# Another order of the setup, and three smaller moves, in a fused attention and expert kernel

## The chip, the cores and the metric

One core of one Trainium2 chip runs the whole kernel. The metric is the device time of one execution in microseconds (us). The kernel before was timed in three runs: 333.94, 334.50 and 335.64 us, median 334.5.

## The reference

There are two stages, and the output of the first is the input of the second.

Attention with a decaying state: 4 batches, 8 heads, 768 tokens, head size 48. For each head, token after token,

```python
cur   = outer(u * k[t], v[t])
y[t]  = r[t] @ (state + cur)
state = w[:, None] * state + outer(k[t], v[t])
```

Mixture of experts on the 3072 tokens with 384 features: logits are `x @ w_gate + modality_bias[modality_id]`; each token goes to the one expert with the largest logit, and gets `gate_w * (relu(x @ w1[e]) @ w2[e])`, with 8 experts of 384 x 1024 and 1024 x 384.

## The kernel before

**Units.** The 768 tokens of a batch are cut into six chunks of 128. A unit is one chunk of one batch; there are 24, numbered so that the four batches of one chunk follow each other. Within a unit the heads are held as four pairs. The state passes from a unit to the one four later.

**What a unit does.** With powers of w in two tables (`powr`, `powk`), GpSimd makes `rc = r * powr` (`decay`, L361) and the state's keys `kt` (`carry`, L368), VectorE makes `kc = k * powk` (`keys`, L399). TensorE multiplies them into 128 x 128 scores per head (`scores`, L440), VectorE multiplies the scores by the causal mask in two halves (`causal`, L454), and TensorE makes y from them and from v, and the state's increment (`values`, L472). The term of u is apart: `rk` is r times k (`own_turned` L393 for units 0 to 3, `own_keys` L383 later), TensorE multiplies it by u (`bonus`, L406) into a number d per token and head, which is copied out of PSUM (`taken`, L415), and d times v is the term `dv` (`own`, L430: eight ScalarE products, in two halves of four heads). For the units in `SHARED` (9 to 13) GpSimd makes the second half of `dv` in one product (`shared`, L423). VectorE adds `dv` to y (`add`, L506), ScalarE squares the sum for a scale (`token`, L512), VectorE makes a power of two of it (`factor`), ScalarE writes the scaled fp16 copy (`high`, L560) and VectorE the rest (`low`, L564). For units in `TURNED`, k is loaded only by token and TensorE transposes it (`keys_turned`, L348).

**Order.** Each engine has one queue and runs it in program order; the order is written out by hand. In iteration i of the main loop (L1266) the work of several units is interleaved: scores of unit i+1, values of unit i, the state copies (or additions) and the addition to y of unit i-1, causal products of i+1, decay of i+3, keys and state keys of i+2. Between them `fill()` takes single steps of longer jobs: gate weights, routing of finished token groups, the list of experts. `plan(i, f)` puts f at the end of iteration i, `mid[i]` between the two halves of `own`. SyncE issues nearly all loads in program order; some wait until a certain number is there (`pace`), so that the loads of later units and the first expert's weights (`raw`, in halves of six pieces, `half`) keep step with the units. A piece is squared for its scale when it has come (`norm`, L972, on ScalarE).

From unit 15 on (`EASED`) the state is added by VectorE, which then also copies d (units 15 and 16; from 17 on d comes by another way, `OWNED`).

**The setup (L85 to L201)** loads the first units, blanks the rows of the buffers that pad each 48 to 64, builds the tables of powers (copy of w L147, scan L148, reciprocals, copies on ScalarE L155 to L159), makes unit 0's operands (L164 to L168), and brings units 0 to 2 to the point where the loop begins. TensorE first multiplies ones (`WARM`, L135), and three more such products stand ahead of unit 1's scores (L446). `blank` (L106) writes zeros by ScalarE.

**The experts.** While the units run, the first expert's weights are brought to two fp16 halves, and tokens that are already routed go through it in slots. After the last unit a loop works through the rest in blocks of 128 tokens. TensorE has hardly a gap from there to the end.

Of the kernel before, what the change touches and what calls it, by code (L numbers as in the profile page):

```python
# [67 lines left out]
class _Kernel:  # L68
# [16 lines left out]
    def setup(self):  # L85
# [4 lines left out]
        nc.sync.dma_start(w[LOW:TOP, :], self.wT.rearrange("j d a -> (j d) a"))  # L90
        uT = c.tile([P, NPR], F32, name="uT")
        self.ud = [c.tile([P, 2 * NPR * P], F32, name=f"ud{q}") for q in range(4)]
# [30 lines left out]
        for i in range(3):  # L123
            self.lines(i, 1)
        wg = c.tile([P, DC * E], F32, name="wgf")
        nc.sync.dma_start(wg, self.wg)
        bias = c.tile([P, 2 * E], F32, name="bias")
        nc.sync.dma_start(bias, self.bias.to_broadcast([P, 2 * E]))
        mod = c.tile([P, 2 * NT // P], I32, name="mod")
        nc.sync.dma_start(mod, self.mod)  # L130
        self.raw_in = wg, bias, mod

# [6 lines left out]
        self.ones = c.tile([P, P], F32, name="ones")  # L139
        nc.vector.memset(self.ones, 1.0)  # L140
# [20 lines left out]
        p64 = pw[:, :, H2 : H2 + 1].rearrange("p a o -> p (a o)")  # L161
        nc.vector.tensor_mul(self.w128, p64, p64)
        self.ub, self.uw = (c.tile([P, NPR, 2], F32, name=n) for n in ("ub", "uw"))
        self.decay(0, NPR, NPR // 2)  # L164
        self.keys(0, 2)
        u = self.ctx_[0]
        nc.vector.tensor_mul(u["rc"][:TOP, NPR // 2 :], u["rT"][:TOP, NPR // 2 :], self.powr[:TOP, NPR // 2 :])
        self.own_turned(0)  # L168
# [16 lines left out]
        nc.gpsimd.memset(self.ub, 0.0)  # L185
        for j, r in enumerate(HALVES):
            nc.gpsimd.tensor_copy(self.ub[r, :, j], uT[r])
        self.keys_turned(1)
        self.causal(0, 0)
        self.causal(0, 1)  # L190
        self.keys(1)
        self.own_turned(1)
# [3 lines left out]
        pst = self.ps_s.tile([P, 512], F32, tag="s", name="psd")  # L196
        self.bonus(0, pst)
        self.taken(0)
        self.carry(1)
        self.feed(3)  # L200
        self.turned(4)  # L201

    def setup2(self):
# [48 lines left out]
    def counts(self):  # L252

        c, v = self.c, self.nc.gpsimd
        self.onesb = c.tile([P, P], BF16, name="onesb")
        v.memset(self.onesb, 1.0)
        self.id16 = c.tile([P, P], F16, name="id16")
        make_identity(self.nc, self.id16)
        self.tok = c.tile([P, NT // P], I32, name="tok")
# [7 lines left out]
        self.base = c.tile([P, E], F32, name="base")  # L267
        v.tensor_copy(self.base, self.cbase)
        self.line = c.tile([P, 1], F32, name="line")
        v.tensor_copy(self.line, self.tok[:, 0:1])  # L270

# [56 lines left out]

    def turned(self, i):
# [5 lines left out]
        self.nc.sync.dma_start(ud[LOW:TOP, :m], self.pd[b * NCH + c].rearrange("j d n -> (j d) n")[:, :m])  # L335
        self.ctx_.setdefault(i, {}).update( rT=ud[:, :n].rearrange("p (a t) -> p a t", a=NPR), kT=ud[:, n:].rearrange("p (a t) -> p a t", a=NPR))
# [23 lines left out]

    def decay(self, i, n=1, of=None):  # L361
        nc, u = self.nc, self.ctx_[i]
        u["rc"] = self.a.tile([P, NPR, P], F32, tag="rc", name=f"rc{i}", bufs=4)
        for q in range(of or n):
            s = slice(q * NPR // n, (q + 1) * NPR // n)
            nc.gpsimd.tensor_mul(u["rc"][:TOP, s], u["rT"][:TOP, s], self.powr[:TOP, s])  # L366

# [24 lines left out]

    def own_turned(self, i):  # L393

        u = self.ctx_[i]
        u["rk"], u["uw"] = self.a.tile([P, NPR, P], F32, tag="rk", name=f"rk{i}"), self.ub
        self.nc.vector.tensor_mul(u["rk"][:TOP], u["kT"][:TOP], u["rT"][:TOP])

    def keys(self, i, n=1):  # L399
        nc, a, u = self.nc, self.a, self.ctx_[i]  # L400
        u["kc"] = a.tile([P, NPR, P], F32, tag="kc", name=f"kc{i}")
        for q in range(n):
            s = slice(q * NPR // n, (q + 1) * NPR // n)
            nc.vector.tensor_mul(u["kc"][:TOP, s], u["kT"][:TOP, s], self.powk[:TOP, s])

# [34 lines left out]
    def scores(self, i):  # L440
        nc, u = self.nc, self.ctx_[i]
        u["ps"] = [self.ps_a.tile([P, 512], F32, tag="big", name=f"psc{i}_{j}") for j in range(2)]
        if i == 1:

            for q in range(DENSE // 2):
                nc.tensor.matmul(u["ps"][q % 2], self.ones16, self.warm, start=True, stop=True)  # L446

        for pr in range(NPR):
            for q in range(2):
                s = slice(64 * q, 64 * q + 64)  # L450
                for j, r in enumerate(HALVES):
                    nc.tensor.matmul(u["ps"][j][s, pr * P : (pr + 1) * P], u["kc"][r, pr, s], u["rc"][r, pr, :], start=True, stop=True)  # L452
# [519 lines left out]
    def norm(self, junk, q):  # L972
        self.nc.scalar.activation(junk, self.raw[:, q * WQ : (q + 1) * WQ], AF.Square, accum_out=self.ssq[:, q : q + 1])
# [191 lines left out]
    def run(self):  # L1165
# [26 lines left out]
        def plan(step, f):  # L1192
            at.setdefault(step, []).append(f)
# [72 lines left out]
        for i in range(NU - 1):  # L1266
            self.step = i
            if i == 0:
                each(i + 5, self.turned)
                each(i + 4, self.lines)  # L1270
            if i < GROUPED:
                each(i + 2, self.keys_turned)
# [336 lines left out]
```

## Time and profile before

| | |
|---|---|
| median of three runs | 334.5 us (333.94 to 335.64) |
| the profiled execution, its own time | 336.65 us |
| its span, first to last instruction | 334.6 us |
| mean granted TensorE clock | 0.994 |
| TensorE busy (products) | 320.0 us, 96% |
| VectorE, ScalarE, GpSimd busy | 213.5, 181.7, 159.7 us |

In a profile a line such as "row L562 <- DVE sx L318" says that the instruction of line 562 that writes the tile row waited, and that VectorE's line 318 released it. PE is TensorE's products, PEld its weight loads, DVE VectorE, ACT ScalarE, POOL GpSimd, SPq SyncE's queue of transfers. "issue" is time in which an engine waited for nothing that the profile shows. The setup and the first iterations take the first 14 us, iteration 4 begins near 26 us, the units end near 170 us.

### The profile page before, as it was taken

The page shows a single profiled execution, that of the slowest core. Times are in us where ns is not written, and L with a number is a line of the kernel's source. Part 1 is how long each engine was busy: PE and PEld are TensorE (multiplying, and loading weights), DVE is VectorE, ACT ScalarE, POOL GpSimd, SP SyncE. Part 2 cuts the span into 40 slices and gives each one's busy share as a digit, 9 for nine tenths or more (in the row PEclk, how much of TensorE's full clock was granted, in tenths as well). Part 3 has the DMA queues.
Part 4 walks back from the last instruction along what each step waited for, and adds up shares of the span by engine and source line. Part 5 has one row for each costly group of instructions (what it writes and reads, how often), then busy time and mean ns, then how long its engine had stood idle before and what let it go on. Part 6 is the DMA issues. An engine that isn't in the chain of part 4 may idle for free. (4 is left out here: it accounts for less than half of the span.)

```text
span 334.6 us, 15202 instructions
## 1 busy us (share of the span) xinstructions
PE 320.0 (96%) x5434; PEld 263.5 (79%) x5434; DVE 213.5 (64%) x727; ACT 181.7 (54%) x500; POOL 159.7 (48%) x241
## 2 busy tenths in 40 slices
PE   7999998998999999999999999999999999999992
PEld 2888897898978888797878788886888877777771
DVE  6878985899988988896667422286333332234950
ACT  7898888789655578676422222274222225543820
POOL 8978863967599886554458212203111111111211
PEclk9999999899999999999999999999999999999999
DMA  6879986995579999954246431119512211122110
GB/s 185 244 171 207 204 250 222 293 229 155 126 197 270 267 223 299 275 156 119 78 106 231 156 78 47 47 47 332 121 50 65 50 47 24 47 56 62 37 47 5
DMA packets 58013, 48.71 MB, mean 146 GB/s; under 512 B 42344, under 2 KB 50807, under 8 KB 57712
## 3 DMA queue, kind: packets, MB, share of 16 engines
q1 hardware_dynamic: 54768, 38.63, 47.5%
q0 software_dynamic: 3200, 9.47, 8.2%
q8 instruction: 30, 0.49, 0.7%
q14 instruction: 15, 0.12, 0.1%
HBM read 27.99 MB, written 11.83 MB: 119 GB/s over the span
## 5 line engine op out<-in xcount | busy, mean ns | idle before, releaser
L1067 PEld LDWEIGHTS <-whi 128*128 128x128 f16 x1248 | 72.6, 98 | 3.6 <-issue 0.7
L1076 DVE SCALAR_TENSOR_TENSOR hl<-phb,hh 128x256 f16<-128x256 f32 (+1 forms) x48 | 24.4, 508 | 66.8 <-ACTq L1540 66.8
L1130 PEld LDWEIGHTS <-hh 128*128 128x128 f16 x416 | 39.1, 98 | 25.3 <-ACT hh L1071 1.2
L1067 PE MATMUL phb<-mxT,whi 128*128 128x128 f16 x768 | 50.7, 219 | 0.0
L438 ACT ACTIVATE dv<-kv,d 128x48 f32<-128x48 f32 x172 | 43.0, 325 | 0.0
L1071 ACT ACTIVATE hh<-phb 128x256 f16<-128x256 f32 (+1 forms) x48 | 21.5, 455 | 32.4 <-PE phb L1067 22.9
L1067 PEld LDWEIGHTS <-wlo 128*128 128x128 f16 x624 | 37.8, 98 | 0.0
L1036 POOL TENSOR_TENSOR seenb<-otb,putb 128x1 int32<-128x1 int32 x16 | 4.1, 257 | 63.0 <-ACTq L1540 50.8
L458 DVE TENSOR_TENSOR at<-psc,mask 128x512 f32<-128x512 f32 x48 | 32.5, 681 | 1.5 <-PE psc L452 1.4
L1130 PEld LDWEIGHTS <-hl 128*128 128x128 f16 x208 | 19.8, 98 | 15.7 <-issue 2.5
L366 POOL TENSOR_TENSOR rc<-ud,powr 112x512 f32<-112x512 f32 (+1 forms) x25 | 30.8, 1237 | 0.2
L1027 ACT ACTIVATE otb<-po,fac 128x384 f32<-128x384 f32 x16 | 9.3, 580 | 39.5 <-PE phb L1067 39.5
L452 PE MATMUL psc<-rc,kc 64*64 64x128 f32 (+1 forms) x768 | 28.5, 281 | 1.2 <-POOL rc L366 1.0
L701 POOL DMA_INDIRECT rows<-row,posi x24 | 24.6, 1026 | 10.2 <-issue 3.6
L1067 PE MATMUL phb<-mxT,wlo 128*128 128x128 f16 x384 | 29.3, 219 | 0.0
L1130 PE MATMUL po<-whi,hl 128*128 128x384 f16 x136 | 28.0, 326 | 1.2 <-PEq L1605 0.7
L1130 PE MATMUL po<-whi,hh 128*128 128x384 f16 x136 | 27.7, 326 | 0.6 <-ACT hh L1071 0.4
L489 PE MATMUL py<-kv,at 128*64 128x48 f32 x768 | 27.0, 222 | 1.2 <-issue 1.2
L1067 PE MATMUL phs<-mxT,whi 128*128 128x128 f16 x432 | 27.3, 219 | 0.6 <-issue 0.6
L1130 PE MATMUL po<-wlo,hh 128*128 128x384 f16 x136 | 27.7, 326 | 0.0
L452 PEld LDWEIGHTS psc<-rc,kc 64*64 64x64 f32 (+1 forms) x768 | 21.9, 135 | 6.5 <-issue 2.5
L489 PEld LDWEIGHTS py<-kv,at 128*64 128x64 f32 x768 | 25.3, 138 | 2.1 <-issue 1.8
(292 smaller groups left out, 625.6 us busy)
## 6 DMA issues: line engine op xcount, KB each, us to landing
kv<-in_pt SPq DMA_DIRECT2D x21, 384.0 KB, 4.8
ud<-in_pd SPq DMA_DIRECT2D x14, 384.0 KB, 5.4
raw<-in_w SPq DMA_DIRECT2D x12, 256.0 KB, 5.1
raw<-in_w SPq DMA_DIRECT2D x6, 512.0 KB, 5.2
raw<-in_w SPq DMA_DIRECT2D x2, 1536.0 KB, 6.5
rows<-pad SPq DMA_DIRECT2D x10, 193.0 KB, 3.6
ud<-in_pd SPq DMA_DIRECT2D x10, 192.0 KB, 3.8
rt<-in_pt SPq DMA_DIRECT2D x7, 192.0 KB, 5.2
```

The costliest lines, as they stand in the source:

```text
L366: nc.gpsimd.tensor_mul(u["rc"][:TOP, s], u["rT"][:TOP, s], self.powr[:TOP, s])
L438: nc.scalar.activation(u["dv"][:, sl], u["v"][:, sl], AF.Copy, scale=u["d"][:, h : h + 1])
L452: nc.tensor.matmul(u["ps"][j][s, pr * P : (pr + 1) * P], u["kc"][r, pr, s], u["rc"][r, pr, :], start=True, stop=True)
L458: nc.vector.tensor_mul(u["at"][:, j * NPR : (j + 1) * NPR, :], u["ps"][j].rearrange("p (q t) -> p q t", q=NPR), self.mask.unsqueeze(1).to_ ...
L489: nc.tensor.matmul(py[t, sl], u["at"][:, j * NPR + pr, t], u["v"][:, sl], start=c == h == 0, stop=h == H - 1, skip_group_check=True)
L701: i = nc.gpsimd.indirect_dma_start(out=self.rows, out_offset=bass.IndirectOffsetOnAxis(ap=u["posi"][:, b : b + 1], axis=0), in_=u["row"][: ...
L1027: self.nc.scalar.activation(ot, po[:, :DM], AF.Copy, scale=gf[:, t : t + 1])
L1036: i1 = nc.gpsimd.tensor_tensor(seen, ot[:, 0:1].bitcast(I32), idx, ALU.add)
L1067: self.nc.tensor.matmul(ph[:, q * P : (q + 1) * P], w[:, c0 : c0 + P], self.xT[:, xq, t * P : (t + 1) * P], start=i == q == 0, stop=i == l ...
L1071: self.nc.scalar.activation(self.hh[:, f0 : f0 + fb, t * P : (t + 1) * P], p3, AF.Relu)
L1076: self.nc.vector.scalar_tensor_tensor(self.hl[:, f0 : f0 + fb, r], p3, 0.0, self.hh[:, f0 : f0 + fb, r], ALU.max, ALU.subtract)
L1130: self.nc.tensor.matmul(po[:, :DM], h[:, f, t * P : (t + 1) * P], w[:, c0 : c0 + DM], start=first, stop=last)
```

## The change

In the setup, unit 0's load is issued from ScalarE's queue, and the load of u becomes four rows of 96, which TensorE transposes and ScalarE copies to `ub` (before: 4-byte elements by the DMA, copies by GpSimd). Some memsets change their engine: `ud[0]` from VectorE to ScalarE, `ud[2]` from ScalarE to GpSimd, `ones` from VectorE to GpSimd. The `kt` blankings move ahead of the tables on ScalarE; those of `ud[3]` and of the state `st[1]` move behind the copy of unit 0's d. Unit 0's operands are made in a new function `first`; `rk` of unit 0 goes to GpSimd. Bonus and d of unit 0 and the transposition for unit 2 move ahead of the setup's end. The loads of the gate weights, bias and modality numbers go behind those of unit 3 (gate) and of unit 4's r (the other two). One warm-up product fewer, and the three ahead of unit 1's scores are left out. Unit 0's scores go through the pairs in the order 0, 1, 3, 2.

Besides: units 1 to 3 join `SHARED`; the squares of the second raw piece go from the end of iteration 8 to the middle of iteration 9; and in units 15 and 16 the copy of d stands ahead of the addition to y.

```diff
-WARM = 10
+WARM = 9
-DENSE = 6
-SHARED = range(9, 14)
+SHARED = (*range(1, 4), *range(9, 14))
...
         self.ones16 = warm[:, :P]
+        self.turned(0, nc.scalar)
+        self.turned(1)
+        ux = c.tile([NPR, TOP], F32, name="ux")
+        self.ub, self.uw = (c.tile([P, NPR, 2], F32, name=n) for n in ("ub", "uw"))
+        nc.gpsimd.memset(ux, 0.0)
+        nc.gpsimd.memset(self.ub, 0.0)
+        nc.sync.dma_start(ux[:, LOW:], self.u.rearrange("o (a z) -> (o a) z", a=NPR))
         for t in self.kv:
             nc.vector.memset(t[:, :LOW], 0.0)
-        nc.vector.memset(self.ud[0][:LOW], 0.0)
...
-        nc.vector.memset(uT, 0.0)
-        blank(self.ud[2][:LOW])
-        self.turned(0)
-        self.turned(1)
-        nc.sync.dma_start(uT[LOW:TOP, :], self.u.rearrange("o (a z) -> z (o a)", a=NPR))
+        blank(self.ud[0][:LOW])
+        for t in self.kt:
+            nc.scalar.copy(t[:, :, :LOW], zero[:, : NPR * LOW].rearrange("p (a z) -> p a z", a=NPR))
...
-        self.counts()
+        nc.gpsimd.memset(self.ud[2][:LOW], 0.0)
+        self.numbers()
...
+        self.first(p64)
         self.decay(1)
+        self.own_turned(0, nc.gpsimd)
         self.scores(0)
...
-        blank(self.ud[3][:LOW])
-        for t in self.kt:
-            nc.scalar.copy(t[:, :, :LOW], zero[:, : NPR * LOW].rearrange("p (a z) -> p a z", a=NPR))
+        self.masks()
+        psd = self.ps_s.tile([P, 512], F32, tag="s", name="psd")
+        nc.tensor.transpose(psd[:TOP, :NPR], ux, id32[:NPR, :NPR])
+        for j, r in enumerate(HALVES):
+            nc.scalar.copy(self.ub[r, :, j], psd[r, :NPR])
+        self.keys_turned(1)
...
+        self.causal(0, 0)
+        self.keys(1)
+        self.causal(0, 1)
+        self.own_turned(1)
+        self.keys_turned(2)
+        self.bonus(0, psd)
+        self.taken(0)
+        blank(self.ud[3][:LOW])
         blank(self.st[1].rearrange("p b a e -> p (b a e)"))
...
+        self.counts()
         self.feed(3)
+        wg = c.tile([P, DC * E], F32, name="wgf")
+        nc.sync.dma_start(wg, self.wg)
         self.turned(4)
+        bias = c.tile([P, 2 * E], F32, name="bias")
+        nc.sync.dma_start(bias, self.bias.to_broadcast([P, 2 * E]))
+        mod = c.tile([P, 2 * NT // P], I32, name="mod")
+        nc.sync.dma_start(mod, self.mod)
+    def first(self, p64):
...
+        part(nc.gpsimd, "rc", "rT", self.powr, slice(NPR - 1, NPR))
+        part(nc.vector, "kc", "kT", self.powk, lo)
+        part(nc.vector, "rc", "rT", self.powr, lo)
+        nc.vector.tensor_mul(self.w128, p64, p64)
+        part(nc.vector, "kc", "kT", self.powk, hi)
+        part(nc.vector, "rc", "rT", self.powr, slice(half, NPR - 1))
...
-        if i == 1:
-            for q in range(DENSE // 2):
-                nc.tensor.matmul(u["ps"][q % 2], self.ones16, self.warm, start=True, stop=True)
-        for pr in range(NPR):
+        for pr in range(NPR) if i else (0, 1, 3, 2):
...
-        for q in range(3):
+        for q in range(0, 3, 2):
             plan(O - 1 + q, norm(q))
+        mid[O + 1] = norm(1)
...
             if i >= EASED:
                 for j in range(2):
                     self.state(i - 1, j)
+                if i not in OWNED:
+                    self.taken(i)
             self.token(i - 1) if i else None
...
-            if i >= EASED:
+            if i in OWNED:
                 self.taken(i)
-                self.shared(i)
```

## Rows read from the trace of the kernel before

**Rows 1.** The page: engines (busy us, share, instructions), queues (packets, MB, share).
```profile
PE 320.0 (96%) x5434; PEld 263.5 (79%) x5434; DVE 213.5 (64%) x727; ACT 181.7 (54%) x500; POOL 159.7 (48%) x241
...
q8 instruction: 30, 0.49, 0.7%
```

**Rows 2.** Timeline of the setup, all but ScalarE: start us, us, engine, line, tiles, count.
```profile
1.27 0.94 POOL L104 MEMSET ud<- 16x1024 f32 x1
...
4.79 1.85 SPq L345 DMA_DIRECT2D kv<-in_pt  x4
...
5.70 2.73 POOL L366 TENSOR_TENSOR rc<-ud,powr 112x128 f32<-112x128 f32 x3
...
6.40 0.45 PE L452 MATMUL psc<-rc,kc 64*64 64x128 f32 x8 [0.56 <-POOL rc L366]
7.25 0.89 PE L452 MATMUL psc<-rc,kc 64*64 64x128 f32 x24 [0.41 <-POOL rc L366]
...
9.09 0.63 PE L413 MATMUL psd<-ub,rk 112*64 112x2 f32 x16
...
10.14 0.81 PE L446 MATMUL psc<-warm 128*128 128x512 f16 x3
...
10.35 1.27 POOL L366 TENSOR_TENSOR rc<-ud,powr 112x512 f32<-112x512 f32 x1
```

**Rows 3.** Timeline of the setup, ScalarE; in brackets the idle time before.
```profile
2.10 1.04 ACT L106 COPY ud<-zero 16x1024 f32<-16x1024 f32 x1
...
4.86 0.41 ACT L159 COPY powr<-powk 128x256 f32<-128x256 f32 x1
...
7.28 0.68 ACT L179 COPY kt<-zero 128x64 f32<-128x64 f32 x4
...
9.14 1.48 ACT L106 COPY st<-zero 128x1536 f32<-128x1536 f32 x1
10.51 0.17 ACT L421 COPY d<-psd 128x8 f32<-128x8 f32 x1
...
14.00 0.64 ACT L544 COPY st<-pst 64x192 f32<-64x192 f32 x2 [1.16 <-PE pst L413]
```

**Rows 4.** Timeline of iterations 1 to 4, all engines.
```profile
17.94 0.56 DVE L510 TENSOR_TENSOR py<-py,dv 128x384 f32<-128x384 f32 x1
...
18.53 0.49 ACT L529 ACTIVATE row<-py 128x384 f16<-128x384 f32 x1
...
19.30 1.28 POOL L391 TENSOR_TENSOR rk<-rc,kc 112x512 f32<-112x512 f32 x1
...
26.55 1.10 PE L452 MATMUL psc<-rc,kc 48*64 48x128 f32 x30 [0.23 <-DVE at L458]
```

**Rows 5.** Line 345, the loads by token, up to 16 us.
```profile
DMA to landing us min/median/max: 3.5/4.5/4.8
```

**Rows 6.** Timeline of iteration 9, 52 to 56 us, all engines.
```profile
53.50 1.06 ACT L973 ACTIVATE junk<-raw 128x1024 f16<-128x1024 f32 x1 [1.42 <-DMA raw<-in_w]
...
54.72 0.55 PE L489 MATMUL py<-kv,at 128*64 128x48 f32 x11 [1.17 <-issue]
...
55.41 0.48 PEld L497 LDWEIGHTS pst<-st,wd 112*64 112x64 f32 x15 [0.27 <-ACT d L421]
...
55.44 0.51 POOL L428 TENSOR_TENSOR dv<-kv,d 128x192 f32<-128x192 f32 x1 [4.77 <-ACT d L421]
```

**Rows 7.** Queues from 51.5 to 53.6 us: packets, MB, share of 16 engines.
```profile
q8 instruction: 1, 0.02, 5.9%
```

**Rows 8.** Timeline of iteration 15, 96.9 to 99 us.
```profile
98.06 0.64 PE L502 MATMUL pst<-kv,kt 128*64 128x48 f32 x16 [0.57 <-DVE d L421]
...
98.73 0.37 PEld L413 LDWEIGHTS pst<-uw,rk 112*64 112x64 f32 x10 [0.16 <-POOL rk L391]
```

**Rows 9.** Stretches (us): length, busy time (count) of each engine, PEclk, DMA share, GB/s.
```profile
5.80:6.40 0.60, 0.04 (x2) 0.01 (x1) 0.60 (x2) 0.60 (x4) 0.60 (x2) 1.00 1.01 331
...
57.20:60.60 3.40, 3.40 (x43) 3.01 (x42) 2.46 (x9) 3.36 (x10) 3.17 (x4) 0.50 0.80 222
```

More of the change, by code (lines that the diff above doesn't have):

```diff
@@ L90, in setup @@
         nc.sync.dma_start(w[LOW:TOP, :], self.wT.rearrange("j d a -> (j d) a"))
-        uT = c.tile([P, NPR], F32, name="uT")
         self.ud = [c.tile([P, 2 * NPR * P], F32, name=f"ud{q}") for q in range(4)]
@@ L124, in setup @@
             self.lines(i, 1)
[L125 to L131, printed above, removed]
         pt = self.ps_a.tile([P, 512], F32, tag="big", name="pwarm")
@@ L139, in setup @@
         self.ones = c.tile([P, P], F32, name="ones")
-        nc.vector.memset(self.ones, 1.0)
+        nc.gpsimd.memset(self.ones, 1.0)
         id32 = self.id32 = c.tile([P, P], F32, name="id32")
@@ L161, in setup @@
         p64 = pw[:, :, H2 : H2 + 1].rearrange("p a o -> p (a o)")
[L162 to L168, printed above, removed]
+        self.first(p64)
         self.decay(1)
+        self.own_turned(0, nc.gpsimd)
         self.scores(0)
@@ L183, in setup @@
         nc.scalar.copy(self.wtok, pt.rearrange("p (a z) -> p a z", a=NPR)[:, :, LOW:TOP])
-        blank(self.st[1].rearrange("p b a e -> p (b a e)"))
[L185 to L192, printed above, removed]
+        self.causal(0, 0)
[6 more added lines that the diff above has]
+        blank(self.ud[3][:LOW])
+        blank(self.st[1].rearrange("p b a e -> p (b a e)"))
         self.carry(0)
@@ L195, in setup @@
         nc.gpsimd.tensor_mul(self.uw, self.ub, w.unsqueeze(2).to_broadcast([P, NPR, 2]))
-        pst = self.ps_s.tile([P, 512], F32, tag="s", name="psd")
-        self.bonus(0, pst)
-        self.taken(0)
         self.carry(1)
+        self.counts()
         self.feed(3)
+        wg = c.tile([P, DC * E], F32, name="wgf")
+        nc.sync.dma_start(wg, self.wg)
         self.turned(4)
+        bias = c.tile([P, 2 * E], F32, name="bias")
+        nc.sync.dma_start(bias, self.bias.to_broadcast([P, 2 * E]))
+        mod = c.tile([P, 2 * NT // P], I32, name="mod")
+        nc.sync.dma_start(mod, self.mod)
+        self.raw_in = wg, bias, mod
+    def first(self, p64):
+        nc, u, half = self.nc, self.ctx_[0], NPR // 2
+        u["rc"] = self.a.tile([P, NPR, P], F32, tag="rc", name="rc0", bufs=4)
+        u["kc"] = self.a.tile([P, NPR, P], F32, tag="kc", name="kc0")
+        part = lambda eng, out, x, pw, s: eng.tensor_mul(u[out][:TOP, s], u[x][:TOP, s], pw[:TOP, s])
+        lo, hi = slice(0, half), slice(half, NPR)
+        part(nc.gpsimd, "rc", "rT", self.powr, slice(NPR - 1, NPR))
[4 more added lines that the diff above has]
+        part(nc.vector, "rc", "rT", self.powr, slice(half, NPR - 1))
     def setup2(self):
@@ L254, in counts, with masks @@
         c, v = self.c, self.nc.gpsimd
+        self.base = c.tile([P, E], F32, name="base")
+        v.tensor_copy(self.base, self.cbase)
+        self.line = c.tile([P, 1], F32, name="line")
+        v.tensor_copy(self.line, self.tok[:, 0:1])
+    def masks(self):
+        c, v = self.c, self.nc.gpsimd
         self.onesb = c.tile([P, P], BF16, name="onesb")
@@ L258, in counts, with numbers @@
         make_identity(self.nc, self.id16)
+    def numbers(self):
+        c, v = self.c, self.nc.gpsimd
         self.tok = c.tile([P, NT // P], I32, name="tok")
@@ L266, in counts @@
         self.idx, self.rev, self.cbase = (ci[:, q] for q in range(3))
[L267 to L270, printed above, removed]
     def setup5(self):
@@ L327, in feed, with turned @@
         self.lines(i)
-    def turned(self, i):
+    def turned(self, i, by=None):
         b, c = self.units[i]
@@ L334, in turned @@
         m = n if i in TURNED else 2 * n
-        self.nc.sync.dma_start(ud[LOW:TOP, :m], self.pd[b * NCH + c].rearrange("j d n -> (j d) n")[:, :m])
+        (by or self.nc.sync).dma_start(ud[LOW:TOP, :m], self.pd[b * NCH + c].rearrange("j d n -> (j d) n")[:, :m])
         self.ctx_.setdefault(i, {}).update( rT=ud[:, :n].rearrange("p (a t) -> p a t", a=NPR), kT=ud[:, n:].rearrange("p (a t) -> p a t", a=NPR))
@@ L359, in pace, with decay @@
         self.nc.values_load(ap[:1].bitcast(I32)[:, :1], engines=SP, skip_runtime_bounds_check_because="the value is not used, only the time at which it is there")
-    def decay(self, i, n=1, of=None):
+    def decay(self, i):
         nc, u = self.nc, self.ctx_[i]
         u["rc"] = self.a.tile([P, NPR, P], F32, tag="rc", name=f"rc{i}", bufs=4)
-        for q in range(of or n):
-            s = slice(q * NPR // n, (q + 1) * NPR // n)
-            nc.gpsimd.tensor_mul(u["rc"][:TOP, s], u["rT"][:TOP, s], self.powr[:TOP, s])
+        nc.gpsimd.tensor_mul(u["rc"][:TOP], u["rT"][:TOP], self.powr[:TOP])
     def carry(self, i):
@@ L391, in own_keys, with own_turned, keys @@
         nc.gpsimd.tensor_mul(u["rk"][:TOP], u["rc"][:TOP], u["kc"][:TOP])
-    def own_turned(self, i):
+    def own_turned(self, i, by=None):
         u = self.ctx_[i]
         u["rk"], u["uw"] = self.a.tile([P, NPR, P], F32, tag="rk", name=f"rk{i}"), self.ub
-        self.nc.vector.tensor_mul(u["rk"][:TOP], u["kT"][:TOP], u["rT"][:TOP])
-    def keys(self, i, n=1):
+        (by or self.nc.vector).tensor_mul(u["rk"][:TOP], u["kT"][:TOP], u["rT"][:TOP])
+    def keys(self, i):
         nc, a, u = self.nc, self.a, self.ctx_[i]
         u["kc"] = a.tile([P, NPR, P], F32, tag="kc", name=f"kc{i}")
-        for q in range(n):
-            s = slice(q * NPR // n, (q + 1) * NPR // n)
-            nc.vector.tensor_mul(u["kc"][:TOP, s], u["kT"][:TOP, s], self.powk[:TOP, s])
+        nc.vector.tensor_mul(u["kc"][:TOP], u["kT"][:TOP], self.powk[:TOP])
     def bonus(self, i, pst):
@@ L1270, in run @@
                 each(i + 4, self.lines)
-            if i < GROUPED:
+            if 0 < i < GROUPED:
                 each(i + 2, self.keys_turned)
```

## The prediction

> **What bounds the kernel now.** I read the page first. TensorE is busy for 96% of the span [rows 1], so the time follows its queue from the first scores to the last product, and an edit is worth only what it takes out of TensorE's waits. Second came the timeline of the setup: TensorE's first scores start at 6.40 us, wait again until 7.25, and from there the queue is nearly closed [rows 2]. Third came the timeline from 14 to 27 us, because TensorE looks full there and yet is led. One chain passes from ScalarE to VectorE and back with no slack: the state of unit 0 (14.00) [rows 3], `high(0)`, `low(0)`, `causal(2)`, the addition of unit 1 (17.94), its squares (18.53), `high(1)`, `low(1)`, `causal(3)`, the addition of unit 2, `causal(4)`, and then TensorE's scores of unit 5, which had waited for it (26.55) [rows 4]. So what a faster setup is worth at 26.55 is what it takes off 14.00, the start of the state copies, and not what it takes off the first scores. Behind 26.55 TensorE's waits are short, up to the two places that the last parts of the change touch.
>
> **The setup.** Three things change for the start of that chain.
>
> First scores. ScalarE gets the issue of unit 0's load ahead of its work, about 0.45 us (four issues of SyncE took 1.85) [rows 2], then the blanking of `ud[0]`, which takes the place of the one that starts at 2.10 and lasts 1.04, then the four `kt` copies (0.68) that stood at 7.28 [rows 3]. The tables can be copied from 2.10 + 0.45 + 1.04 + 0.68 - 0.2 (each starts about 0.1 before the one ahead ends) = 4.1. With three copies of 0.41 `powr` is whole at 5.1 to 5.3, against 4.86 + 0.41 = 5.27 before [rows 3]. What VectorE saves ahead of its scan (a memset of the shape that takes GpSimd 0.94 [rows 2], above all) is not passed on: ScalarE comes to the tables at 4.1 in any case. The gain is in what follows: VectorE itself multiplies r of the first two head pairs, and TensorE starts at about 5.7 instead of 6.40, without the second wait of 0.41 [rows 2].
>
> Unit 0's bonus. It needs three things. GpSimd: its queue ahead of the decays loses four small instructions and a wait and gains a memset of 0.94; I take it to be free when `powr` is there (5.2) or, at worst, at the 5.70 of before. The three products there took 2.73; now it is a whole one of 1.27 more and a quarter less, so 3.2, which gives 8.4 to 9.0 [rows 2]. The lines of unit 2: issued 0.5 to 1.0 earlier than 4.79 (unit 0's issue has left SyncE's queue, and the load of u waits for less), landed 3.5 to 4.8 after that [rows 5], and then a transposition of 10.14 - 9.09 - 0.63 = 0.4: 7.7 to 9.5. TensorE itself: 9.09 - 6.40 - 0.41 = 2.28 us of work from the first scores to the bonus before [rows 2], and the transpositions of unit 2 and of u besides, 0.6: 5.7 + 2.9 = 8.6. I take 8.6, which lies between all three, and keep 8.3 and 9.2 as ends.
>
> State of unit 0. In the profile ScalarE copied d at 10.51, was done with its eight products and the gate's squares 2.33 us later, and then sat idle for 1.16 until 14.00, released by TensorE [rows 3]. Now the blankings of `ud[3]` (1.04, by its twin) and of the state (1.48) stand between d and those products, where before they filled idle time. The bonus takes 0.63 [rows 2], so d starts at 8.6 + 0.7 = 9.3, and ScalarE is free for the state at 9.3 + 1.04 + 1.48 + 2.33 - 0.3 = 13.85. TensorE has the data over a microsecond earlier, so this step is now ScalarE's own. The gain is 14.00 - 13.85 = 0.15, with ends of 0.45 faster and 0.45 slower. The three dense products (0.81) [rows 2] and the earlier scores are hidden: TensorE is early and waits at `causal(2)` and, by over a microsecond, at `causal(3)`.
>
> The other loads only move: kv of unit 3 goes ahead of the gate's weights, which are wanted at 13.5. The bias and the modality numbers wait behind `turned(4)`, which waits for GpSimd (8.6); they are read in iteration 3. I cost these at nothing, as the chain covers them; if one were late, ScalarE's queue would stop there, and with it everything behind 14.00.
>
> Of the queue that unit 0's load takes, the Trainium skill ("DMA: Bandwidth & Descriptors", "Issuing engines are not separate DMA queues") says that DMAs of all issuing engines run on the same 16 DMA engines and interleave, and only the time of the issue is saved. By that the load gains one slot of SyncE and can hold up w beside it. No row here shows two such queues at once; the sum has no gain from it.
>
> **Half of d v on GpSimd, units 1 to 3.** ScalarE loses four products in each of three iterations; GpSimd gets 0.51 us each [rows 6]. The four that go are those behind `high`, and the next link of the chain, the squares, waits for the addition on VectorE and not for them (17.94 + 0.56 = 18.50, squares at 18.53) [rows 4]. So they are worth nothing at 26.55. GpSimd is 1.5 us behind after the three halves: its `rk` of unit 4, which ended at 20.58, ends at about 22, and the bonus that reads it stands just ahead of the scores at 26.55 [rows 4]. Ends: 0.4 faster (if ScalarE's share does count before `causal(4)`) and 0.3 slower.
>
> **Squares of the second raw piece.** ScalarE waits 1.42 us for the raw data and squares at 53.50; the state copies and d of unit 9 stand behind that [rows 6]. After the move they go first. But TensorE stands still from about 53.5 to 54.72 with no engine named, "issue" [rows 6]: in this stretch one instruction packet takes 5.9% of 16 engines over 2.1 us [rows 7], 1.98 us, against a mean of 0.7% x 16 x 334.6 / 30 = 1.25 [rows 1]. I read the stop as TensorE's own instructions arriving late behind the raw data. Only then does it wait for d, from 54.72 + 0.55 = 55.27 to 55.41. So the wait that is removed lies beside another, and the step is worth 0.15. Ends: 0, and 55.41 - (53.5 + 0.55) = 1.3 if both stops go.
>
> **d ahead of the addition, units 15 and 16.** TensorE waits 0.57 us for d at 98.06. But right behind, at 98.73, the bonus waits for GpSimd's `rk` [rows 8]; with d earlier the same engine waits for GpSimd until the same 98.73. In unit 16 no such wait shows. Worth 0; ends 0.57 faster and 0.1 slower (the squares of unit 14, behind a later addition).
>
> **The sum.** 0.15 + 0 + 0.15 + 0 = 0.3 us less than the profiled execution's 336.65 (span 334.6 and 2.05 around it): 336.35. That execution is 2.15 above the median of 334.5, and I carry the difference over: 334.2. The three runs lie 1.7 apart, so about 0.5%, 1.7 us, is what a measurement can tell from no change.
>
> **Rivals.**
> *The second stop and the clock go too.* Behind the stop of 53.5 the granted clock is 0.50, which is 1.2 GHz, from 57.20 to 60.60 [rows 9]; that costs half of 3.4, 1.7 us. If the stop was ScalarE's wait in truth, or if its end keeps the clock up, the time is 334.2 - 1.7 = 332.5 with the clock alone and 334.2 - 1.15 - 1.7 = 331.35 with both. For it: the stop begins where ScalarE's wait ends. Against: the instructions that TensorE resumes with need nothing of ScalarE, and a median run may not have the fall of the clock at all. Chance 0.30.
> *TensorE at 1.2 GHz in the setup: slower.* One warm-up product less, no dense ones, and a new idle time of over a microsecond at `causal(3)`. If the clock comes up late, or falls as after the stop of 53.5, a stretch like that of rows 9 takes 1.7 us from TensorE. In the setup this decides as soon as TensorE reaches the bonus later than GpSimd does (8.4 to 9.0), thus almost at once: d at 9.3 + 1.7 = 11.0, state at 15.55, 1.55 us later than before: 334.5 + 1.55 - 0.15 = 335.9. For it: the one long idle time of the profile was followed by 0.50. Against: TensorE also stood idle from 5.80 to 6.40, and the clock reads 1.00 there [rows 9]. Chance 0.15. The Trainium skill ("TensorE: Matmul & The Clock Gate", "What's actually happening") puts this as "the default state is throttled, and activity releases the throttle".
> *The loads lead.* Unit 2's lines land at the late end, or the first load holds up w: bonus at 9.2 or later, state at 14.45 or later: 334.8 to 335.3. Chance 0.10.
>
> **Chances and range.** My forecast has 0.45. Of the first rival nearly all is faster by over 0.5% (0.28), with a little from my own case (0.04): 0.32. Of the slower rival, and of late loads on top of it, 0.10 passes 0.5%. Within 0.5%: 0.58. The range takes in the clock alone on one side (332.0) and the slow setup on the other (335.9); outside are the case of 331.35 (0.13) and two slow stretches (0.05). The forecast's own range is 333.0 to 335.0.
>
> **What would show it.** Right: first scores near 5.7, ScalarE's state copies near 13.85 directly behind its own work, TensorE waiting at `causal(3)`, scores of unit 5 near 26.4; in iteration 9 no wait of ScalarE for raw data but still a TensorE stop marked "issue"; at unit 15 the bonus waiting for `rk`. Wrong: scores of unit 5 over a microsecond earlier (then the chain is not rigid, or the share on GpSimd counts), no stop near 53, or a granted clock of 0.50 before 26 us.

## The result and the profile after

The kernel after takes 339.19 us (median of 6 runs, 336.94 to 340.97), the kernel before 334.72 beside it (6 runs): a ratio of 1.0131, 95% interval 1.0084 to 1.0179. It is slower by 1.3%. I had forecast 334.2 us and no measurable change; the result lies outside my range.

The profiled execution of after takes 338.89 us (span 337.0). Its timeline, with the lines that answer to [rows 2 to 4] (start us, us, engine, line, operation, tiles, count; in brackets the idle time ahead and what ended it):

```profile
0.81 0.40 ACTq L356 DMA_DIRECT2D ud<-in_pd  x1
...
0.98 0.41 SPq L89 DMA_DIRECT2D w<-in_wT  x1
...
1.39 3.80 PE L131 MATMUL pwarm<-warm 128*128 128x512 f16 x9 [1.39 <-POOL warm L97]
...
4.54 0.29 DVE L143 COPY tables<-w 128x256 f32<-128x256 f32 x1 [2.68 <-DMA w<-in_wT]
...
7.37 1.42 PE L464 MATMUL psc<-rc,kc 64*64 64x128 f32 x24 [2.18 <-DVE rc L207]
...
7.59 1.52 POOL L385 TENSOR_TENSOR rc<-ud,powr 112x512 f32<-112x512 f32 x1
...
7.91 1.35 DVE L207 TENSOR_TENSOR rc<-ud,powr 112x128 f32<-112x128 f32 x1
...
9.32 0.71 PE L464 MATMUL psc<-rc,kc 64*64 64x128 f32 x8 [0.53 <-DVE rc L207]
9.95 0.25 PE L170 MATMUL psd<-id,ux 4*112 4x4 f32 x1
10.13 1.10 PE L375 MATMUL pkT<-id,kv 128*112 128x128 f32 x4
...
12.88 1.02 PE L430 MATMUL psd<-ub,rk 112*64 112x2 f32 x16
...
13.94 0.17 ACT L438 COPY d<-psd 128x8 f32<-128x8 f32 x1 [1.34 <-PE psd L430]
...
14.01 1.04 ACT L110 COPY ud<-zero 16x1024 f32<-16x1024 f32 x1
14.95 1.47 ACT L110 COPY st<-zero 128x1536 f32<-128x1536 f32 x1
...
19.10 0.64 ACT L556 COPY st<-pst 64x192 f32<-64x192 f32 x2 [0.67 <-PE pst L430]
...
22.99 0.56 DVE L522 TENSOR_TENSOR py<-py,dv 128x384 f32<-128x384 f32 x1
...
23.58 0.49 ACT L541 ACTIVATE row<-py 128x384 f16<-128x384 f32 x1
...
31.72 1.10 PE L464 MATMUL psc<-rc,kc 48*64 48x128 f32 x30 [0.35 <-DVE at L470]
```

The lines of before for the same steps, as far as they aren't in the rows:

```profile
0.97 0.41 SPq L90 DMA_DIRECT2D w<-in_wT  x1
...
2.98 0.23 DVE L147 COPY tables<-w 128x256 f32<-128x256 f32 x1
...
8.07 0.66 PE L182 MATMUL pwk<-id,wk 128*128 128x128 f32 x4
```

Read it from the end. Unit 5's scores start at 31.72 against 26.55, 5.17 us later [rows 4]; the state copies of unit 0 at 19.10 against 14.00, 5.10 later [rows 3]. So all that unit 5 loses is there at 19.10, and the chain between passes it on almost unchanged. Upwards: d is copied at 13.94 (10.51 before), the bonus starts at 12.88 (9.09), the first scores at 7.37 (6.40), and VectorE stands idle for 2.68 us until w has landed and copies it at 4.54. Nothing was issued late: SyncE sends w's load at 0.98 (0.97 before). But ScalarE now sends unit 0's load ahead of it, at 0.81.

The second thing to see is TensorE's pace. The bonus's 16 products take 1.02 us instead of 0.63, four transpositions 1.06 to 1.10 instead of 0.60 to 0.66. The stretches of after (length, busy time and count of PE, PEld, DVE, ACT, POOL, then PEclk, DMA share, GB/s), to be held against [rows 9]:

```profile
1.39:4.40 3.01, 3.01 (x8) 1.08 (x9) 0.40 (x3) 2.76 (x6) 2.93 (x11) 1.00 0.84 229
...
8.30:18.40 10.10, 9.57 (x129) 8.13 (x126) 6.25 (x10) 5.97 (x19) 8.38 (x13) 0.50 0.57 168
18.50:26.50 8.00, 8.00 (x219) 7.26 (x218) 5.62 (x13) 6.41 (x25) 5.71 (x8) 1.00 0.56 131
57.20:60.60 3.40, 3.40 (x118) 3.38 (x116) 2.71 (x9) 3.33 (x14) 2.46 (x3) 1.00 0.86 283
73.10:76.40 3.30, 3.30 (x44) 2.91 (x41) 2.99 (x2) 3.24 (x12) 3.21 (x5) 0.50 0.84 256
```

For ten microseconds from 8.30 on TensorE is granted half its clock, 1.2 GHz. A granted clock of 0.50 before 26 us is one of the signs of being wrong that the prediction names. Later the two executions differ in the other direction: the stretch of 57.2 to 60.6 is at full clock here and has one like it at 73.1.

### The profile page after: what moved, and what is told of

It reads as the page before. It is cut to its first block, busy times and chain, and to the rows that moved or that the text cites. A ratio compares the mean times of both kernels' runs of the same rounds, so it can differ in the third digit from the quotient of the medians.

```text
span 337.0 us, 15194 instructions
## 1 busy us (share of the span) xinstructions
PE 321.6 (95%) x5431; PEld 265.7 (79%) x5431; DVE 214.4 (64%) x724; ACT 179.1 (53%) x490; POOL 164.2 (49%) x245
## 3 DMA queue, kind: packets, MB, share of 16 engines
q1 hardware_dynamic: 54264, 38.24, 46.6%
HBM read 27.99 MB, written 11.83 MB: 118 GB/s over the span
## 5 line engine op out<-in xcount | busy, mean ns | idle before, releaser
L455 ACT ACTIVATE dv<-kv,d 128x48 f32<-128x48 f32 x160 | 40.0, 325 | 0.0
L464 PE MATMUL psc<-rc,kc 64*64 64x128 f32 (+1 forms) x768 | 29.5, 290 | 3.3 <-DVE rc L207 2.7
L713 POOL DMA_INDIRECT rows<-row,posi x24 | 25.6, 1066 | 9.3 <-issue 3.4
L385 POOL TENSOR_TENSOR rc<-ud,powr 112x512 f32<-112x512 f32 x23 | 29.7, 1291 | 0.2
L1021 DVE SCALAR_TENSOR_TENSOR wlo<-raw,ws,whi 128x1024 f16<-128x1024 f32 (+1 forms) x20 | 25.9, 1317 | 1.4 <-issue 0.7
```

The lines of the kernel that those rows point to most:

```text
L385: nc.gpsimd.tensor_mul(u["rc"][:TOP], u["rT"][:TOP], self.powr[:TOP])
L455: nc.scalar.activation(u["dv"][:, sl], u["v"][:, sl], AF.Copy, scale=u["d"][:, h : h + 1])
L713: i = nc.gpsimd.indirect_dma_start(out=self.rows, out_offset=bass.IndirectOffsetOnAxis(ap=u["posi"][:, b : b + 1], axis=0), in_=u["row"][: ...
L1021: self.nc.vector.scalar_tensor_tensor(self.wlo[:, sl], self.raw[:, sl], sc, self.whi[:, sl], ALU.mult, ALU.subtract)
```

## The experiments

My theory: unit 0's load, on a second queue, overtakes w; the tables come late; TensorE idles behind its warm-ups and the clock falls; the blankings behind d add to it. The rivals are named with each run. Three chips were used, on which the kernel before takes 335.5, 340.1 and 339.8 us, so I compare ratios to the runs of before beside them. Of the profiled executions four times are enough:

| kernel | ratio to before, 95% interval | w copied | d | state copies | scores of unit 5 |
|---|---|---|---|---|---|
| before | 1 | 2.98 | 10.51 | 14.00 | 26.55 |
| after | 1.0131, 1.0084 to 1.0179 | 4.54 | 13.94 | 19.10 | 31.72 |
| e1 load behind w | 0.9975, 0.9938 to 1.0012 | 2.66 | 11.88 | 16.29 | 28.81 |
| e2 load alone | 1.0092, 1.0058 to 1.0125 | 4.58 | 11.97 | 18.16 | 30.71 |
| e3 bridge | 1.0045, 1.0010 to 1.0079 | 4.50 | 11.93 | 16.33 | 28.86 |
| e4 old setup | 0.9977, 0.9942 to 1.0011 | 2.99 | 9.98 | 13.80 | 26.49 |
| e5 blanks ahead | 1.0051, 1.0003 to 1.0099 | 2.65 | 13.59 | 16.59 | 29.25 |
| e6 dense | 1.0049, 1.0010 to 1.0087 | 2.69 | 11.83 | 14.59 | 27.26 |
| e7 no dense | 0.9995, 0.9953 to 1.0038 | 2.98 | 9.92 | 13.47 | 26.19 |
| e8 norm alone | 0.9971, 0.9937 to 1.0006 | 2.98 | 9.87 | 13.68 | 26.23 |
| e9 old setup, thin | 1.0024, 0.9984 to 1.0063 | 2.99 | 9.93 | 13.49 | (a late load) |
| e10 bridge, blanks | 1.0026, 0.9990 to 1.0062 | 4.49 | 12.17 | 15.02 | 27.68 |
| e11 mended setup | 1.0035, 1.0002 to 1.0067 | 2.65 | 12.27 | 15.34 | 27.95 |
| e12 after again | 1.0111, 1.0062 to 1.0160 | 4.45 | 13.67 | 18.08 | 30.61 |

**e1: the load behind w.** On the kernel after:

```diff
-        self.turned(0, nc.scalar)
+        self.turned(0)
```

> The kernel after, with unit 0's load issued by SyncE right behind the load of w, instead of by ScalarE; nothing else. Theory (w is overtaken): in the trace after, VectorE waits 2.68 us for w and copies it at 4.54, the tables, the first scores (7.37) and all that follows are late, and TensorE, idle from 5.2 on, is granted 0.5 from 8.2 to 18.5. With w on its old place VectorE copies w by 3.0, the first scores start at 5.5 to 6.0, the granted clock stays 1.0 up to 26 us, the state copies of unit 0 come at 13.5 to 14.2 instead of 19.10, and the time is 331.5 to 333.5. Rival A (nine warm-up products and no dense ones are too little, whenever the tables come): w comes early too, but the clock still falls before 26 us, the state copies stand at 15.5 or later, and the time stays above 335. Rival B (the blankings behind d, or GpSimd's longer queue, hold the state up): clock 1.0, but the state copies at 15 or later and 334.5 to 336.

```profile
2.66 0.29 DVE L143 COPY tables<-w 128x256 f32<-128x256 f32 x1 [0.80 <-DMA w<-in_wT]
...
5.80 1.21 PE L464 MATMUL psc<-rc,kc 64*64 64x128 f32 x24 [0.92 <-DVE rc L207]
...
7.75 0.71 PE L464 MATMUL psc<-rc,kc 64*64 64x128 f32 x8 [0.73 <-DVE rc L207]
...
16.29 0.62 ACT L556 COPY st<-pst 64x192 f32<-64x192 f32 x2
```

This one word takes the ratio from 1.0131 to 0.9975. w is copied at 2.66, and the first scores start at 5.80, within 0.1 of what the prediction had. But the time missed its expectation (334.74 against 331.5 to 333.5): the clock still reads 0.50 from 7.6 to 11.0, and the state copies come at 16.29. So the clock and the state of rival A came true, though not its time, and of rival B the blankings, behind which ScalarE goes to the state without a pause: there is more wrong in the new setup than w. e5, e6 and e11 carry the same edit among others and have 1.0035 to 1.0051, so what is shown is that most of the loss goes with the load's old queue, not that nothing is left.

**e2: the load alone.** On the kernel before:

```diff
         self.ones16 = warm[:, :P]
+        self.turned(0, nc.scalar)
...
-        self.turned(0)
         self.turned(1)
```

> The kernel before, with one edit: unit 0's load issued by ScalarE ahead of its work, as in the kernel after; ten warm-up products and six dense ones stay, and all else. Theory (the load on a second queue overtakes w): VectorE waits over 1 us for w, copies it between 4.2 and 4.8 instead of 2.98, the first scores start at 7.5 to 8.2 instead of 6.40, state copies of unit 0 at 15.2 or later instead of 14.00, and the time rises by 1 us with the clock kept and by up to 5 with a fall of the clock: 335.5 to 340. Rival A (w is late only through other edits of the setup, such as the second load right behind it): w copied by 3.2, scores by 6.4, and the time is that of before within 1 us.

```profile
4.58 0.31 DVE L147 COPY tables<-w 128x256 f32<-128x256 f32 x1 [1.52 <-DMA w<-in_wT]
...
18.16 0.64 ACT L544 COPY st<-pst 64x192 f32<-64x192 f32 x2 [3.87 <-PE pst L413]
```

With ten warm-ups, the three dense products (`DENSE // 2`) and the old order of everything else, the moved load alone costs 0.92%. Its clock reads 0.50 from 9.3 to 16.0, and its state copies are 4.16 us late. The rival falls.

How the load does it is in the DMA view. First after from 1.8 to 3.0 us, then before from 1.9 to 2.4 (packets; then by queue: packets, MB, share of 16 engines):

```profile
DMA packets 77, 0.32 MB, mean 263 GB/s; under 512 B 0, under 2 KB 0, under 8 KB 77
...
q10 hardware_dynamic: 77, 0.32, 89.2%
```

```profile
DMA packets 112, 0.00 MB, mean 3 GB/s; under 512 B 112, under 2 KB 112, under 8 KB 112
...
q1 hardware_dynamic: 112, 0.00, 10.4%
```

Before, 112 packets under 512 bytes, w's among them, are through by 2.4. After, until 3.0 the 16 engines carry nothing but the other queue's large packets, 0.32 of unit 0's 0.39 MB; SyncE's queue has not moved one. So 0.17 us of lead in the issue became 1.56 us at the copy of w (4.54 to 2.98), or 1.88 against e1, where VectorE waits for w too and copies it at 2.66. The Trainium skill ("DMA: Bandwidth & Descriptors", "Queues, rings and completion order") says that each engine takes turns between the queues, a whole packet at a time; its packet is a group of descriptors. The trace agrees only if the seven profile packets of unit 0's load that fall to an engine (112 over 16) are one such group, which no view shows: nearly five of the seven went ahead of w's first.

**e3 and e10: the clock, then the blankings.** e3 is the kernel after with `WARM = 14`; e10 moves ScalarE's blankings besides:

```diff
             wk.append(t)
+        blank(self.ud[3][:LOW])
...
+        blank(self.st[1].rearrange("p b a e -> p (b a e)"))
         nc.scalar.copy(self.wtok, ...)
...
-        blank(self.ud[3][:LOW])
-        blank(self.st[1].rearrange("p b a e -> p (b a e)"))
```

> The kernel after, with 14 warm-up products in place of 9, so that TensorE is busy to about 7.4, where the first scores start; w stays late. This tells the price of the clock apart from that of the late tables. Theory (the idle stretch between the warm-ups and the scores lets the clock fall): the granted clock stays 1.0 up to 26 us; the bonus of unit 0 comes at 10.4 to 11.2 instead of 12.88, the state copies at 15.3 to 16.3 instead of 19.10, and the time is 334 to 336. Rival (the gaps behind the first scores, 1.1 us at 8.2 and 0.5 at 9.4, make it fall whatever stands ahead): 0.5 again within 8 to 20 us, state copies at 18 or later, time above 337.

> The kernel after with 14 warm-ups, as in the bridged run, and ScalarE's two blankings ahead of d of unit 0. In the bridged run the clock was 1.0 throughout the setup, d was copied at 11.93, the state copies came at 16.33 behind ScalarE's own work, the addition of unit 0 at 16.25, and scores of unit 5 at 28.86. Theory (the blankings are 2.4 us on the chain from d to the state once d is late): clock 1.0, d at 11.9 to 12.1, state copies at 14.4 to 15.1, the addition at 13.9 to 14.6, scores of unit 5 at 27.0 to 27.8, and 1 to 1.8 us less than the bridged run, whose ratio to before was 1.0045: 0.999 to 1.002. Rival (TensorE is as late as ScalarE, so the blankings cost nothing): state copies after 15.8, unit 5 at 28.5 or later.

The state copies of e3, then of e10:

```profile
16.33 0.62 ACT L556 COPY st<-pst 64x192 f32<-64x192 f32 x2
```

```profile
15.02 0.64 ACT L556 COPY st<-pst 64x192 f32<-64x192 f32 x2 [0.53 <-PE pst L430]
```

w is as late as in after (4.50, 4.49), but the 14 warm-ups keep TensorE busy until the scores in e3 and until 1.01 us ahead of them in e10. Both setups are at full clock: PEclk reads 1.00, and four transpositions take 0.60 to 0.65 us, as in e3:

```profile
10.28 0.60 PE L176 MATMUL pwk<-id,wk 128*128 128x128 f32 x4
```

In e3 the state copies follow ScalarE's own work without a pause; in e10 they wait for TensorE again. This splits the 5.10 us: 19.10 - 16.33 = 2.77 is the clock, 16.33 - 15.02 = 1.31 the blankings behind d, and 15.02 - 14.00 = 1.02 the late w and the new order. The ratios follow (1.0131, 1.0045, 1.0026), though the last two don't differ by more than their intervals, and e3's time (336.79) is above the 334 to 336 that I expected. The shares are those of single executions, taken in this order: in e12, the same kernel as after, the state copies come at 18.08, by which the clock's share is 1.75.

**e7: no dense products.** On the kernel before, `WARM = 9` and `DENSE = 0`.

> The kernel before with nine warm-ups instead of ten and without its six dense products ahead of unit 1's scores (they write what the scores overwrite); all else as before. My prediction's slower rival blamed the missing products for the clock. If they alone decide: granted clock 0.50 within 8 to 20 us, state copies of unit 0 at 15 or later instead of 14.00, time 336 or more. If it is the late w that opens the idle stretch: clock 1.0 up to 26 us, state copies at 13.9 to 14.2, time that of before within 0.5 us.

Nothing is lost (0.9995). The state copies come at 13.47, not later than in e4 and e8 (13.80 and 13.68), whose old setup is untouched, and four transpositions take 0.60 to 0.66 us. So in the old setup the missing products, which I had blamed in my slower rival, do not bring the clock down; a late w does, even with all products there (e2). In the new setup it goes by the products, and not by w. Of its executions the four with nine warm-ups (after, e12, e1, e5) are at half pace somewhere between 7.6 and 18.5 us, e1 and e5 with an early w; the four with ten and dense products or with 14 (e6, e11, e3, e10) are not, e3 and e10 with a late one.

**e4 and e8: the small parts.** e4 is the kernel before with the three small parts and its old setup; e8 has the move of the squares alone.

> The kernel before with the three small parts of the change and its old setup: half of d v on GpSimd in units 1 to 3, the second raw piece's squares in mid iteration 9, d ahead of the addition in units 15 and 16. Theory, from where unit by unit the kernel after wins back 2.4 of the 5.05 us that its setup lost: the stop of TensorE at 53.3 to 54.7 was the wait for raw data, so it goes (1.4 to 1.8 us), and with it the fall of the clock at 57.2 in executions that have one; unit 7 gains 0.5 or nothing from the share on GpSimd; unit 15 nothing. Time 332 to 333.3. Rival, my prediction's own view (the stop is instructions that arrive late, and stays): 334.2 to 334.8, with an idle time of over 1 us in iteration 9 still there.

> The kernel before with one edit: the squares of the second raw piece in mid iteration 9. With the old setup and all three small parts, TensorE's stop of 1.38 us in iteration 9 was gone, one of 0.87 stood in iteration 8, and unit 11 came 0.75 us earlier. If the raw wait was the cause and the other two parts are worth nothing: the same here within 0.3 us up to unit 11, no stop over 0.6 us between 52 and 55, time 0.5 to 1.5 below before. Rival (the stop is instructions that arrive late): a stop of over 1 us marked issue in iteration 8 or 9, and unit 11 within 0.4 us of before.

Iteration 9 of e8 (with [rows 6]), and the queue from 51.9 to 53.8 us (with [rows 7]):

```profile
55.36 0.44 PE L489 MATMUL py<-kv,at 128*64 128x48 f32 x9 [1.20 <-issue]
...
55.48 1.05 ACT L973 ACTIVATE junk<-raw 128x1024 f16<-128x1024 f32 x1
```

```profile
q8 instruction: 1, 0.02, 5.8%
```

In e8 ScalarE no longer waits for raw data, and TensorE stops for 1.20 us all the same. e4, with the same move, has a stop of 0.66 in iteration 8 and none in iteration 9; e7, without it, has none in either. So the move does not decide it. An instruction packet goes ahead of each stop; it takes 5.8% x 16 x 1.9 us = 1.76 in e8 and 1.79 ahead of e4's, but 1.30 in e4's iteration 9 and 1.25 in after (5.6% x 16 x 1.4), where TensorE doesn't stop. I took its slowness for the cause, and other traces speak against that. In e10 the longest stop is behind a packet of 5.3% x 16 x 1.2 = 1.02 (the stop, then the queue from 46.6 to 47.8 us), and in e7 there is none behind one of 5.9% x 16 x 2.6 = 2.45 (from 42.9 to 45.5).

```profile
49.27 0.33 PE L509 MATMUL pst<-st,wd 112*48 112x48 f32 x5 [1.62 <-issue]
```

```profile
q8 instruction: 1, 0.02, 5.3%
```

What the stops have in common is when they end: the fourteen traces hold 30 such stops of 0.4 us or more between 30 and 140 us, and in each TensorE goes on 1.2 to 1.7 us behind the end of an instruction packet. That fits instructions that arrive late; why most packets cause no stop stays open. Neither ratio can be told from 1, nor is either far from it: 0.9977 and 0.9971.

**e5, e6, e9 and e11: repairs.** e5 is e1 with e10's move of the blankings. e6 adds to it a tenth warm-up and eight dense products in TensorE's waits. e11 changes e6: VectorE takes r of both last pairs, four dense products instead of eight, the transposition of u just ahead of the bonus, the pairs in their old order, the blanking of the state by GpSimd. e9 is e4 with `WARM = 9` and `DENSE = 0`.

> The kernel after with unit 0's load on SyncE behind w, and also the two blankings of ScalarE (1.04 and 1.47 us) back ahead of d of unit 0: that of ud[3] behind the four wk products, that of the state ahead of the copy of wtok, where ScalarE idled for 1.26 and 1.50 us in the run with only the load moved. There d was copied at 11.88 and the state copies came at 16.29, behind ScalarE's own work. Theory (the blankings are a term of their own, 2.4 us on the chain from d to the state, hidden only if the bonus is as early as 9): d at 11.7 to 12.3, the state copies at 14.2 to 15.0, scores of unit 5 1.2 to 2.2 us earlier than the 28.81 of that run, time 1 to 2 us less than that run had (334.74 median). Rival (TensorE at 1.2 GHz, or GpSimd's rk, holds the state anyway): state copies at 15.8 or later and no gain.

> As the run before this one, with ten warm-ups instead of nine and eight dense products of 512 columns that only fill TensorE's waits among the first scores (two at 6.1, four at 6.6, two at 7.9). Theory (idle stretches among the scores let the clock fall at 7.6 to 11.0): granted clock 1.0 up to 26 us, the bonus at 9.6 to 10.4 instead of 11.20, state copies at 13.0 to 14.0, so level with the kernel before or earlier by up to 1.0 (scores of unit 5 at 25.5 to 26.6); time 331.5 to 333.5 and below every kernel so far. Rival (the clock's fall does not hang on these waits, or the bonus waits for u's load and GpSimd): a granted clock of 0.50 again before 20 us, or the bonus at 11 or later, and no gain over the run before.

> The kernel after with its setup mended: unit 0's load on SyncE behind w; ten warm-ups and four dense products ahead of the third head pair; VectorE multiplies r of both last pairs (in the trace after GpSimd does one, and VectorE's single pair takes 1.35 us beside GpSimd's decay); the transposition of u ahead of the bonus instead of ahead of unit 1's lines (TensorE waited there for u's load until 8.4 to 9.9); the blanking of ud[3] ahead of d; the blanking of the state by GpSimd. Theory (w, the clock, the blankings and u's load are all that was wrong): clock 1.0 up to 26 us, first scores at 5.8 to 6.0, d at 10.0 to 10.8, state copies at 13.0 to 13.8, scores of unit 5 at 25.6 to 26.4, ratio 0.993 to 0.998. Rival (the new order itself loses, for instance GpSimd's decay of unit 1 ahead of rk of unit 0): state copies at 14.5 or later and a ratio of 1.000 or more.

> The kernel before with the three small parts of the change, and of its new setup only what is taken away from TensorE: nine warm-ups and no dense products (these write what is overwritten). The run without the products had unit 1's scores 0.53 us and the state copies of unit 0 0.53 us earlier (13.47) at full clock; the run of the old setup with the three parts had the rest. Theory: state copies near 13.5, scores of unit 5 0.3 to 0.4 earlier than 26.55, and a time of 0.3 to 0.6% below before. Rival (these differences are within what one execution differs from the next): a ratio of 0.998 or more.

All miss their expected times. In e5 w is early, yet TensorE is at half pace until 13 us (three groups of four transpositions from 10.10 on take 1.06 to 1.10 each), and d is at 13.59; from d to the state it takes 3.00 us instead of e1's 4.41: the blankings are out of the way. e6 keeps full pace, but has its bonus at 10.90 and not by 10.4: VectorE is done with the last pair of the first scores at 7.79, my dense products hold TensorE until 8.38, and two more of them and the transpositions of u, of two units and of the decay stand between that pair and the bonus. e9's profiled execution lost its lead to a load that landed late (TensorE waited 1.56 us for it at 26.54). In e11 it is VectorE again:

```profile
5.69 1.27 POOL L384 TENSOR_TENSOR rc<-ud,powr 112x512 f32<-112x512 f32 x1 [0.16 <-DMA ud<-in_pd]
5.73 1.25 DVE L211 TENSOR_TENSOR w<-tables 128x4 f32<-128x4 f32 x1
...
7.23 1.49 DVE L207 TENSOR_TENSOR rc<-ud,powr 112x256 f32<-112x256 f32 x1
...
8.78 0.67 PE L465 MATMUL psc<-rc,kc 64*64 64x128 f32 x16 [0.61 <-DVE rc L207]
...
11.60 0.63 PE L429 MATMUL psd<-ub,rk 112*64 112x2 f32 x16 [0.56 <-ACT ub L184]
```

A product of four columns takes 1.25 us and ends with GpSimd's, which began 0.04 before it; the last pairs come at 8.78, and the bonus, with u's transposition moved next to it, waits 0.56 us for ScalarE's copy of u. The wait for u's load that the expectation speaks of is not there: in after u's transposition follows the scores at 9.95 without a pause. So no version of the new setup is shown to be faster than the old one, and none of the twelve kernels to be faster than the kernel before.

**e12: after again.**

> The kernel after, unchanged, once more, beside the mended ones on one chip: its loss of 1.3% and the fall of the clock in its setup should come again (w copied at 4.4 to 4.6, granted clock 0.50 within 8 to 20 us or not up before 10, state copies at 17.5 to 19.5, ratio 1.008 to 1.018). If the loss belongs to single executions or to one chip: w copied by 3.2, or a ratio below 1.004.

Its setup at 10 us, and the stretch from 8.3 to 13.2 us:

```profile
10.04 1.10 PE L375 MATMUL pkT<-id,kv 128*112 128x128 f32 x4
```

```profile
8.30:13.20 4.90, 4.51 (x41) 3.42 (x35) 3.58 (x6) 1.43 (x6) 3.18 (x6) 1.00 0.75 201
```

The loss is there again, on the chip where the kernel before takes 339.8. The clock column reads 1.00 here, but four transpositions take 1.10 us, as they do in after at 0.50: TensorE is at 1.2 GHz. The first change of the clock that this trace holds is at 13.27 (13.02 in e5, 4.83 in after), and ahead of it the column reads 1.00 at either pace. So in e12 and e5, whose nine warm-ups take 4.02 us (3.80 in after), the clock did not fall; it had not come up before.

## Why the prediction was wrong

**The step that failed** is the landing of w, which I costed at nothing: "What VectorE saves ahead of its scan ... is not passed on: ScalarE comes to the tables at 4.1 in any case". That holds with w on its old place only: ScalarE is at the tables at 3.72 in e1, and at 5.60 in after, 1.45 of it a wait for VectorE's scan. I saw that the first load "can hold up w beside it", filed it as a late load with 0.10, and priced it at 0.3 to 0.8 us. Moved alone it costs 4.16 us at the state copies (e2). What I should have asked: two queues, one of them without a wait in front; which load reaches the engines first, and what stands behind it?

**The slower rival had the clock, and neither all of its cause nor its size.** "TensorE at 1.2 GHz in the setup" is what happened, with its chance of 0.15. It named the missing products, with which the clock goes in the new setup, and not the late w, which is enough in the old one (e2). I priced one stretch like that of [rows 9], 1.7 us; it lasted over 10 us and cost 2.77 (1.75 by e12). And I argued against it that the clock reads 1.00 from 5.80 to 6.40 [rows 9]. That reading was empty: in after nine warm-ups of 512 columns take 3.80 us, 0.42 each, while PEclk reads 1.00 from 1.39 to 4.40; three dense products of the same size took 0.81, 0.27 each [rows 2]. Before the first change in a trace (6.03 in before) the column tells nothing, and the durations do.

**The bonus at 8.6** was wrong even with w and the clock in order. I let TensorE's 2.9 us of work follow the first scores "without the second wait of 0.41"; there was a longer one, for the last pair, on which VectorE spent 1.35 us beside GpSimd. With w early that pair starts at 7.75 (e1), and at full pace the bonus comes 1.98 behind it (9.27 to 11.25 in e3): 9.7 as an estimate, over a microsecond late. e6's 10.90 holds dense products besides.

**ScalarE's part was right.** I had 9.3 to 13.85, 4.55 us, from d to the state with the blankings between; e1, e3 and e12 show 4.41, 4.40 and 4.41. My figure cost nothing only because I believed in d at 9.3: each microsecond that d is late takes the blankings out of hiding.

**The chain was right.** From the state copies to unit 5's scores it took 12.55 us before, and 12.52 to 12.72 in the twelve others that have both times. Behind unit 5 not all of the loss is kept in these two: of 5.17 us after shows 1.3% of 334.7, 4.4; of 2.31 e3 shows 1.5.

**The small parts were right as far as can be told.** Half of d v on GpSimd: e4 has unit 5's scores at 26.49, 0.06 from before; e8, which differs from before only later, has 26.23, so 0.3 us is within what executions differ. The stop marked "issue" stays without ScalarE's wait (e8), and its end fits instructions that arrive late, though a slow packet is not what it hangs on. And at unit 15, in the trace after, the bonus waits for `rk` as foretold [rows 8]:

```profile
101.47 0.63 PE L430 MATMUL pst<-uw,rk 112*64 112x2 f32 x16 [0.61 <-POOL rk L410]
```

**What stays open.** e1 loses 2.26 us at unit 5 and yet has 0.9975; e6 loses 0.71 and has 1.0049, its profiled execution among its quickest. What their other executions did behind unit 5 no trace shows. TensorE is at half pace from 7.6 to 11.0 in e1 and until 13 in e5, with nine warm-ups and an early w in both; no run with an early w changes the warm-ups alone, so which of the missing products counts there isn't settled either.

## What to carry to other kernels

When a load is moved to another queue, list what is then in flight beside it in the order of arrival, and look for a small load that everything waits for: here 0.17 us of lead on another queue put 0.32 MB in front of it. A stretch costed at nothing because something hides it needs its cover checked at the late end too, since one late input can uncover several at once. And an engine's pace is read from the durations of like instructions, not from a clock column.

## What the runs showed of the hardware

VectorE's and GpSimd's products can exclude each other. In after a VectorE product of 112x128 started at 7.91 and took 1.35 us, ending 0.15 after GpSimd's (7.59 + 1.52), where twice the size took 0.42 at 6.89; in e11 four columns took 1.25. The Trainium skill ("SBUF — State Buffer", "Who interferes with whom") says that a VectorE instruction with two inputs in SBUF and a GpSimd instruction that reads SBUF share an interface, and that the one issued second waits. The trace agrees: in both places VectorE's was the second by its start. Moving a product to VectorE "beside" GpSimd bought nothing here (d at 12.27 in e11 and 11.83 in e6, which differ in more than this).
